# The last group without its unread state, and the two halves of the last output block in the other order

## The chip, the cores and the metric

The kernel runs on one core of a Trainium2 chip. The metric is device time in microseconds (us) of one execution: 551.74 us, the median of three runs (549.87 to 553.06). The engines are TensorE (PE: matmuls, with PEld its weight loads), VectorE (DVE), ScalarE (ACT), GpSimd (POOL) and SyncE (SP), which issues transfers. They run side by side and meet at semaphores.

## The reference

Two stages follow each other: a gated linear recurrence with complex gates, and a feed-forward layer that takes the maximum over three products. B = 4, H = 8 heads, S = 768 steps, D = 48; 3072 tokens of 384 features, 768 hidden features.

```python
mag = np.sqrt(a_re * a_re + a_im * a_im)
scale = np.minimum(mag, 0.999) / (mag + 1e-06)
a_re_n, a_im_n = (a_re * scale, a_im * scale)
for t in range(S):
    new_re = ar * S_re - ai * S_im
    new_im = ar * S_im + ai * S_re
    kv = np.einsum('bhd,bhe->bhde', k[:, :, t], v[:, :, t])
    S_re, S_im = (new_re + kv, new_im)
    y[:, :, t] = np.einsum('bhd,bhde->bhe', q[:, :, t], S_re)
x = y.transpose(0, 2, 1, 3).reshape(B * S, H * D)
h = np.maximum(np.maximum(x @ w1, x @ w2), x @ w3)
return h @ w_out
```

The state `S_re`, `S_im` is read in its own step and carried into the next; after the last step nobody reads it.

## The kernel before, in words

The 768 steps are cut into 12 groups (`NG`) of 64. A group has two units, x and y (`C` = 2), each with two of the four batch rows, 64 steps of each on one half of the 128 partitions. For a group the kernel works out the logarithms of the gates' magnitudes (`Ln`) and their angles, turns q and k by the angles, takes the products inside the group (`A`, `B`), adds what comes from the state before the group (`y` with `QG` and `gs`), and adds the group's own keys and values to the state (`dk`, `h0`, `h1`). Then comes the feed-forward layer of the group: `U01`, `U11`, `U02`, `U12` are products of 128x256 with the three weights, with the maxima `u..` behind them, and the product with `w_out` is split in Strassen's manner into seven: `S1` to `S4` are the sums before it on DVE, `P1` to `P7` the products on PE, `r1` to `r57`, `ox`, `oy`, `oz` the additions into the output tile `ot` behind it, and `Dx`, `Dy`, `Dz` the output transfers. `Px` and `Py` are the products of the one block of features that stays outside the split.

The order of everything is written out by hand in the string `SCHEDULE` (line 21): each word is a step, a colon and the group. The class `Bound` (line 189) ties every instruction of an engine to the one before it, so that each engine runs its instructions in just that order; this is also why all of them carry line 198. PSUM tiles of two banks come from `banks` (line 208), whose four slots follow the string `SLOTS` (line 116).

The steps that the change touches:

- `sums` (line 623, in `turns`): per unit, products of `Ln` with two constant matrices. `mid` gives the decay between each step and the middle of its block of eight; `rest` the decay from that middle to the end of the group. Each is four products of 64x192; all go to one PSUM tile, side by side.
- `Ek`, `Eq`, `En` (line 631): exponentials of these sums on ACT. `Ek` and `Eq` read the columns of `mid` and scale k and q (`mk`, `mq`). `En` reads the columns of `rest`.
- `kEn` (line 656): DVE multiplies the turned keys `uk` by `En`, after the transposes `tpk` have read them. The result is read by `dk` alone, the group's own share of the state. For the last group, number 11, `SCHEDULE` has no `dk`, `h0` or `h1`, but before the change it has `Eny:11`, `Enx:11`, `kEnx:11` and `kEny:11`.
- `oy` and `oz` (line 943, in `seven`): in every other group `oy` adds a PSUM bank of 384 columns into the y half's output tile. In the last group `oy` adds the lower 192 columns, into which `P4` and `Py` are summed, and `oz` the upper 192, into which only `Py` is. Both read the second bank of the tile `op7`. The upper half of `ot` is complete ahead of `oz` with `r57`, the lower half ahead of `oy` with `r7`; both of these wait for `P7`.
- `Dy` and `Dz` (`D` in `project`, line 948): the output transfers of these halves in the last group, 64 rows of 192 columns (48 KB) each on the queue of SP and on that of ACT:

```python
queue = act if ch and g == NG - 1 else sp
cols = halves if g == NG - 1 and c == 1 else slice(0, DM)
queue.dma_start(out=out[t0:t0 + L64, cols], in_=T["ot", x][ch * L64:(ch + 1) * L64, cols])
```

The end of `SCHEDULE` before the change reads:

```
u02:11 Dy:10 S3:11 P1:11 r1:11 P2:11 S1:11 S2:11 P5:11 S4:11 P6:11 kEny:11 P3:11 r6:11 r5:11 ox:11 P7:11 P4:11 r7:11
r57:11 Dx:11 oy:11 Dy:11 oz:11 Dz:11
```

The last group's `sums` stand in the middle of work on groups 8 to 10: `sumsy:11` between `dk` and `P3:8`, `sumsx:11` between `dk` and `cs:11`.

Of the kernel before, what the change touches and what calls it, by code (L numbers as in the profile page):

```python
# [97 lines left out]
g2x:9 g3x:9 S3:8 tpkx:10 u12:8 mqx:10 b1y:9 b1x:9 b0x:9 sumsy:10 F:10 Kcx:10 yx:9 S1:8 f3:10 f1:10 addw:11 Eqy:10 xx:9  # L98
h0x:9 S2:8 mqy:10 P5:8 f0:10 f2:10 QGy:9 Eky:10 uqx:10 Lvx:10 lnw:11 kEnx:9 P7:8 Lvy:10 Px:8 P2:8 P6:8 Py:8 half:11
expL:11 mulai:11 uqy:10 P4:8 r1:8 mulw:11 Eny:10 Lky:10 mky:10 r6:8 r5:8 r7:8 r57:8 Lnop:11 oy:8 yy:9 S4:8 tpqx:10  # L100
dkx:9 kEnx:10 h1x:9 xy:9 sumsy:11 stt:11 Eky:11 Cdx:10 Qcx:10 P3:8 uky:10 ox:8 atan:11 Eny:11 Lvx:11 Eqy:11 Lvy:11
U11:9 KBx:10 h0x:10 tpky:10 h0y:10 tpqy:10 Cdy:10 dkx:10 turn:11 Lqy:11 u11:9 kEny:10 Q1x:10 mqy:11 Kcy:10 dky:10
h1x:10 sumsx:11 Qcy:10 cs:11 t:11 h1y:10 nfy:11 nfx:11 F:11 f3:11 Dy:8 Q2y:10 Lqx:11 Ekx:11 U12:9 f1:11 u12:9 QGx:10
S3:9 Lkx:11 mkx:11 U01:9 Q2x:10 f2:11 Eqx:11 af:11 mqx:11 Q1y:10 u01:9 Enx:11 U02:9 QBx:10 Bx:10 Ax:10 u02:9 Ay:10
S1:9 g0x:10 f0:11 P1:9 g1x:10 sb:11 KBy:10 g2x:10 Dx:8 g3x:10 b1x:10 g0y:10 P5:9 g1y:10 Lky:11 mky:11 sa:11 P7:9
QBy:10 g2y:10 g3y:10 S2:9 Py:9 b0x:10 yx:10 xx:10 By:10 b0y:10 P6:9 QGy:10 Px:9 S4:9 P2:9 r1:9 uqy:11 r6:9 P3:9 P4:9
uqx:11 uky:11 r5:9 r7:9 b1y:10 r57:9 yy:10 ox:9 tpqy:11 oy:9 ukx:11 tpqx:11 Qcy:11 xy:10 Q2y:11 tpky:11 Qcx:11 QBx:11
tpkx:11 U01:10 Q2x:11 Q1x:11 Q1y:11 U11:10 u01:10 Kcx:11 KBx:11 Kcy:11 QGy:11 U02:10 u02:10 Bx:11 QBy:11 KBy:11 u11:10
Ax:11 Ay:11 g0y:11 By:11 Dy:9 g0x:11 U12:10 g1y:11 g2y:11 g3y:11 b0y:11 b1y:11 yy:11 S3:10 g1x:11 g2x:11 Dx:9 u12:10
g3x:11 P1:10 Py:10 QGx:11 P4:10 b1x:11 P7:10 S1:10 S2:10 b0x:11 xy:11 Py:11 P5:10 S4:10 yx:11 P6:10 xx:11 r1:10 r6:10  # L110
r5:10 kEnx:11 Px:10 Px:11 P2:10 U11:11 r7:10 r57:10 oy:10 P3:10 ox:10 U01:11 Dx:10 u11:11 U12:11 u12:11 U02:11 u01:11
u02:11 Dy:10 S3:11 P1:11 r1:11 P2:11 S1:11 S2:11 P5:11 S4:11 P6:11 kEny:11 P3:11 r6:11 r5:11 ox:11 P7:11 P4:11 r7:11
r57:11 Dx:11 oy:11 Dy:11 oz:11 Dz:11
"""

SLOTS = """
# [17 lines left out]
def kernel(  # L134
# [25 lines left out]
    NG = S // L64  # L160
# [47 lines left out]
    def banks(nm, n=None):  # L208

        ps = psum.tile([P, 2, 512], FP, tag="ps" + next(slots), name=nm)  # L210
        T["ps"] = ps
        return ps if n is None else ps.rearrange("p a n -> p (a n)")[:, 0:n]
# [4 lines left out]
    def activation(func, **kw):  # L217

        need = SETS.get(func, T.get("set"))
        if need != T.get("set"):  # L220
            act.preload_act_table_set(need)
            T["set"] = need
        act.activation(func=func, **kw)
# [5 lines left out]
    def copy(out, in_):  # L229

        if other():
            dve.tensor_copy(out=out, in_=in_)
        else:
            act.copy(out=out, in_=in_)
# [15 lines left out]
    def once(key, make):  # L250

        if key not in T:
            T[key] = make()
        return T[key]
# [12 lines left out]
    def ones(name, *shape):  # L267
        t = const.tile([P, *shape], FP, name=name)
        dve.memset(t, 1.0)
        return t  # L270
# [10 lines left out]
    mid = ones("mid", L64)  # L281

    rest = ones("rest", L64)
# [99 lines left out]
    def every(view, j):  # L383

        return view.rearrange("p (i u d) -> p i u d", u=2, d=D)[:, :, j]
# [84 lines left out]
    def two(t):  # L470
        n = t.shape[1] // D
        return t.rearrange("p (h u d) -> p h u d", u=1, d=D).to_broadcast([P, n, 2, D])

    def both(t, h):

        return t[:, h]

    def sines_of(t):

        dims = [list(d) for d in t[:, :, 0:D].ap]  # L480
        return bass.AP(t.tensor, t.offset, dims[:-1] + [[L64, 2], dims[-1]])

    def hd(t):
        return t.rearrange("p c h d -> p (c h d)")
# [135 lines left out]
    def turns(g, c, name):  # L620

        x = g * C + c
        if name == "sums":
            ps = T["sums", x] = banks("sums")
            for n, mat in enumerate((mid, rest)):
                for j in range(2):
                    for ch in range(2):
                        r = slice(ch * L64, (ch + 1) * L64)
                        mm(out=ps[j * L64:(j + 1) * L64, ch, n * HC:(n + 1) * HC], lhsT=mat[r],
                           rhs=every(T["Ln", g][r, c * DM:(c + 1) * DM], j), start=True, stop=True)  # L630
        elif name in ("En", "Ek", "Eq"):
            n, sg = {"En": (1, -1.0), "Ek": (0, 1.0), "Eq": (0, -1.0)}[name]
            E = T[name, x] = nat2.tile([P, DM], FP, tag=name[:1 + (n == 1)], name=name[:1 + (n == 1)])
            activation(out=E.rearrange("p (c n) -> p c n", c=2), in_=T["sums", x][:, :, n * HC:(n + 1) * HC],
                           func=AF.Exp, scale=sg)
        elif name in ("mk", "mq"):
            t = hd(T[name[1], x])
            dve.tensor_tensor(out=t, in0=T["E" + name[1], x], in1=t, op=OP.mult)
        elif name in ("uk", "uq"):
            u = T["U" + name[1], x] = us[name[1]][x % len(us[name[1]])]  # L640
            dve.tensor_tensor(out=sines_of(u), in0=T["CS", g][:, c], in1=two(hd(T[name[1], x])), op=OP.mult)
        elif name in ("tpk", "tpq"):
            ps = banks("tp").rearrange("p j (n t) -> p j n t", t=L64)
            T[name, x] = ps[0:DD]
            for n in range(H):
                for j in range(2):
                    r = slice(j * L64, (j + 1) * L64)
                    pe.transpose(out=ps[0:DD, j, n], in_=both(T["U" + name[2], x], n)[r], identity=ident[r, r])
        elif name == "Kc":
            T["K", x] = un2.tile([P, H, P], FP, tag="K", name="K")  # L650
            copy(out=T["K", x][0:DD].rearrange("p n (j t) -> p j n t", j=2), in_=T["tpk", x])
        elif name == "Qc":
            T["Q", x] = un2.tile([P, 4 * H, 80], FP, tag="Q", name="Q")
            copy(out=T["Q", x][0:DD, :, 0:32].rearrange("p (n j a) t -> p j n a t", n=H, j=2),
                 in_=T["tpq", x].rearrange("p j n (a t) -> p j n a t", a=2))
        elif name == "kEn":
            u = sines_of(T["Uk", x])
            dve.tensor_tensor(out=u, in0=u, in1=two(T["En", x]), op=OP.mult)
        elif name == "F":
            tile_sums(g, c)  # L660
        elif name[0] == "f" and name[1:].isdigit():
            tile_factors(g, [c], int(name[1:]))
        else:
            return False
        return True

    def tile_sums(g, c):

        ps = once(("Fp", g, c if g == 0 else "xy"), lambda: banks("F"))
        T["F", g * C + c] = fs[g % 2][:, c]  # L670
        for i in range(2):
            for j in range(2):
                for u in range(2):
                    h, o = 2 * (2 * i + u) + j, u * L64
                    for ch in range(2):
                        r = slice(ch * L64, (ch + 1) * L64)
                        at = (4 * (c if g > 0 else 0) + 2 * i + j) * NF
                        mm(out=ps[o:o + D, ch, at:at + NF],
                           lhsT=T["Ln", g][r, c * DM + h * D:c * DM + (h + 1) * D], rhs=cuts[r],
                           start=True, stop=True)  # L680

    def tile_factors(g, cs, name):

        i, u = divmod(name, 2)
        o, n = i * L64, len(cs)
        ps = T["Fp", g, cs[0] if g == 0 else "xy"][u * L64:u * L64 + D, :, 0:4 * n * NF]
        ps = ps.rearrange("p h (c i n) -> p c h i n", c=n, i=2)
        out = fs[g % 2][o:o + D, cs[0]:cs[0] + n]
        out = out.rearrange("p c (h i u) j n -> p c h i u (j n)", h=2, u=2)[:, :, :, :, u]
        if n == 1:  # L690
            out, ps = out[:, 0], ps[:, 0]
        activation(out=out, in_=ps, func=AF.Exp, scale=-1.0)
# [337 lines left out]
    for c in range(C):  # L1030
        for nm, src in (("ar", a_re), ("ai", a_im)):
            t = once((nm, 0), lambda: ld2.tile([P, C, H, D], FP, tag=nm, name=nm))
# [38 lines left out]
```

## Time and profile before

| what | value |
|---|---|
| median of 3 runs | 551.74 us |
| the runs | 551.74, 549.87, 553.06 us |
| the profiled execution | 552.02 us, its span 550.3 us |
| mean granted TensorE clock | 0.978 |
| last TensorE instruction ends | about 546.2 us in the span |
| bytes moved | 47.93 MB |

The span runs from the first to the last instruction of the profiled execution; its time holds some 1.7 us around it. In the profile's rows an operation is named by its output and inputs (`sums<-Ln,rest`), with the shape and how many of it; a product shows as two rows. The number in square brackets is the time that the engine was idle before, and what ended it; "issue" means that it waited for nothing that the profile shows. `wo` and `w` are names of the weight tiles, `strassen` the tile of the sums before the products, `xhx` the features.

### The profile page before, as it was taken

The numbers are of one execution on the slowest core, as the hardware profiler recorded it, in microseconds if no ns is written. First come the engines' busy times: TensorE is split into PE (matmuls) and PEld (weight loads), VectorE is DVE, ScalarE is ACT, GpSimd is POOL, SyncE is SP. The second block draws the span as 40 slices with busy tenths as digits, with TensorE's granted clock in tenths as the row PEclk, the third lists the DMA queues.
The fourth block names the chain that finished last, engine by engine and source line by source line (L and its number), as shares of the span: only waits on it lengthen the run. The fifth ranks groups of instructions, "written<-read, shape, count | busy, mean of one in ns | idle before, by whom it ended". The sixth has DMA issues, their size and how long they took to land.

```text
span 550.3 us, 22368 instructions
## 1 busy us (share of the span) xinstructions
PE 515.6 (94%) x9998; PEld 441.4 (80%) x9998; DVE 484.8 (88%) x735; ACT 363.8 (66%) x568; POOL 115.6 (21%) x167
## 2 busy tenths in 40 slices
PE   2478989999999999999999999999999899999996
PEld 1245578778988888988898988988988788988886
DVE  7999989999999999999999999988999687886325
ACT  6999898688989778696492638677678465221000
POOL 7524180030251222214004001303101250000000
PEclk9769899999999999999999999999999899999999
DMA  8978975553443455244516025356150350010011
GB/s 233 243 206 170 244 129 89 101 92 69 80 89 74 96 111 104 49 91 83 104 42 121 3 52 107 64 105 112 22 104 11 66 117 2 4 30 4 2 29 29
DMA packets 117023, 47.93 MB, mean 87 GB/s; under 512 B 103936, under 2 KB 109536, under 8 KB 116928
## 3 DMA queue, kind: packets, MB, share of 16 engines
q1 hardware_dynamic: 104272, 31.87, 27.4%
q0 software_dynamic: 10304, 14.05, 14.1%
q8 instruction: 78, 1.28, 0.9%
q10 hardware_dynamic: 2352, 0.59, 0.5%
q14 instruction: 17, 0.14, 0.1%
HBM read 33.03 MB, written 4.72 MB: 69 GB/s over the span
## 4 chain that ended last, share of the span: by engine, by line
PE 71%; DVE 10%; issue 2%; ACT 1%; DVEq 0%; ACTq 0%
PE up L198 28%; PE op L198 22%; PE y L198 6%; PE tp L198 4%; PE A L198 3%; PE dk L198 3%; PE sums L198 2%; DVE atm L198 1%; PE B L198 1%; DVE Q L198 1%; PE F L198 1%; DVE QG L198 1%; PE cs L198 1%; DVE uk L198 1%; DVE xhx L198 1%
## 5 line engine op out<-in xcount | busy, mean ns | idle before, releaser
L198 PE MATMUL up<-xhx,w 128*128 128x256 f32 x792 | 177.5, 382 | 0.0
L198 PEld LDWEIGHTS up<-xhx,w 128*128 128x128 f32 x792 | 148.6, 190 | 22.4 <-DVE g L198 2.2
L198 ACT ACT_TABLE_LOAD x50 | 64.2, 1283 | 4.4 <-issue 3.6
L198 POOL DMA_DIRECT2D ar<-nf x44 | 39.9, 1297 | 77.8 <-DVE ar L198 66.7
L198 ACT COPY atm<-B 32x128 f32<-32x128 f32 x96 | 24.5, 256 | 39.4 <-DVE atm L198 24.2
L198 PE MATMUL op<-wo,xhx 128*128 128x192 f32 (+1 forms) x220 | 49.2, 362 | 0.0
L198 DVE TENSOR_TENSOR Q<-Q,f 112x1024 f32<-112x1024 f32 (+1 forms) x48 | 45.3, 951 | 0.4 <-ACT Q L198 0.2
L198 PE MATMUL y<-atm,vb 128*32 128x64 f32 x1152 | 39.4, 221 | 2.9 <-issue 2.9
L198 PEld LDWEIGHTS op<-wo,xhx 128*128 128x128 f32 x220 | 36.7, 190 | 3.3 <-issue 0.6
L198 PEld LDWEIGHTS y<-atm,vb 128*32 128x32 f32 x1152 | 33.1, 110 | 7.3 <-issue 6.2
L198 PE MATMUL y<-QG,g 112*32 112x64 f32 x1408 | 37.3, 220 | 0.5 <-issue 0.5
L198 DVE TENSOR_TENSOR ot<-ot,op 128x192 f32<-128x192 f32 (+1 forms) x67 | 27.1, 413 | 11.0 <-PE op L198 6.2
L198 DVE TENSOR_TENSOR xhx<-xhx,up 128x768 f32<-128x768 f32 x22 | 20.9, 951 | 17.9 <-PE up L198 17.9
L198 PEld LDWEIGHTS y<-QG,g 112*32 112x32 f32 x1408 | 34.6, 110 | 0.7 <-issue 0.7
L198 PE MATMUL op<-wo,strassen 128*128 128x192 f32 x176 | 34.2, 339 | 0.1
L198 POOL DMA_DIRECT2D w<-L x8 | 9.0, 1124 | 117.4 <-ACT L L198 104.8
L198 PE MATMUL op<-w,strassen 128*128 128x192 f32 x176 | 32.8, 329 | 0.0
L198 DVE COPY_PREDICATED atm<-masko,A 128x256 f32<-128x256 uint8 x72 | 31.2, 435 | 1.2
L198 PEld LDWEIGHTS op<-wo,strassen 128*128 128x128 f32 x176 | 30.0, 196 | 2.3 <-issue 0.7
L198 PE MATMUL A<-Q,K 112*32 112x80 f32 x1536 | 30.6, 234 | 0.5 <-issue 0.5
L198 PEld LDWEIGHTS op<-w,strassen 128*128 128x128 f32 x176 | 28.9, 190 | 1.9 <-ACT ot L198 0.8
L198 PEld LDWEIGHTS A<-Q,K 112*32 112x32 f32 x1536 | 27.4, 110 | 3.6 <-issue 1.4
(156 smaller groups left out, 1114.5 us busy)
## 6 DMA issues: line engine op xcount, KB each, us to landing
ai<-in_a_im_dram SPq DMA_DIRECT2D x46, 96.0 KB, 3.4
ar<-in_a_re_dram SPq DMA_DIRECT2D x46, 96.0 KB, 3.3
out_dram<-ot SPq DMA_DIRECT2D x45, 96.0 KB, 3.0
Ln<-e POOLq DMA_DIRECT2D x10, 384.0 KB, 5.7
q<-in_q_dram SPq DMA_DIRECT2D x34, 96.0 KB, 3.3
k<-in_k_dram SPq DMA_DIRECT2D x32, 96.0 KB, 3.6
w<-L POOLq DMA_DIRECT2D x8, 384.0 KB, 5.0
w<-in_moe_w_dram SPq DMA_DIRECT2D x3, 768.0 KB, 7.0
```

The source lines that it names most:

```text
L198: ins = f(*a, **kw)
```

## The change

The last group's sums lose their `rest` half; its exponentials `En` and its products `kEn` are taken out of the order; and at the end `oz` and `Dz` stand ahead of `oy` and `Dy`. The lines of `SCHEDULE` are wrapped anew, without another change of order. The words taken out, with their neighbours, and the end:

```diff
-atan:11 Eny:11 Lvx:11
+atan:11 Lvx:11
...
-u01:9 Enx:11 U02:9
+u01:9 U02:9
...
-r5:10 kEnx:11 Px:10
+r5:10 Px:10
...
-P6:11 kEny:11 P3:11
+P6:11 P3:11
...
-Dx:11 oy:11 Dy:11 oz:11 Dz:11
+Dx:11 oz:11 Dz:11 oy:11 Dy:11
```

```diff
         if name == "sums":
             ps = T["sums", x] = banks("sums")
-            for n, mat in enumerate((mid, rest)):
+            for n, mat in enumerate((mid, rest) if g < NG - 1 else (mid,)):
```

On the engines that is 8 products fewer on PE, 2 exponentials fewer on ACT and 2 multiplications fewer on DVE, of 9998 rows, 568 and 735 instructions. The table loads of ACT and the orders of POOL and SP stay the same but for the two halves at the end.

More of the change, by code (lines that the diff above doesn't have):

```diff
@@ L100 @@
 expL:11 mulai:11 uqy:10 P4:8 r1:8 mulw:11 Eny:10 Lky:10 mky:10 r6:8 r5:8 r7:8 r57:8 Lnop:11 oy:8 yy:9 S4:8 tpqx:10
[L101 to L113, printed above, removed]
+dkx:9 kEnx:10 h1x:9 xy:9 sumsy:11 stt:11 Eky:11 Cdx:10 Qcx:10 P3:8 uky:10 ox:8 atan:11 Lvx:11 Eqy:11 Lvy:11 U11:9
@@ new lines @@
+KBx:10 h0x:10 tpky:10 h0y:10 tpqy:10 Cdy:10 dkx:10 turn:11 Lqy:11 u11:9 kEny:10 Q1x:10 mqy:11 Kcy:10 dky:10 h1x:10
+sumsx:11 Qcy:10 cs:11 t:11 h1y:10 nfy:11 nfx:11 F:11 f3:11 Dy:8 Q2y:10 Lqx:11 Ekx:11 U12:9 f1:11 u12:9 QGx:10 S3:9
+Lkx:11 mkx:11 U01:9 Q2x:10 f2:11 Eqx:11 af:11 mqx:11 Q1y:10 u01:9 U02:9 QBx:10 Bx:10 Ax:10 u02:9 Ay:10 S1:9 g0x:10
+f0:11 P1:9 g1x:10 sb:11 KBy:10 g2x:10 Dx:8 g3x:10 b1x:10 g0y:10 P5:9 g1y:10 Lky:11 mky:11 sa:11 P7:9 QBy:10 g2y:10
+g3y:10 S2:9 Py:9 b0x:10 yx:10 xx:10 By:10 b0y:10 P6:9 QGy:10 Px:9 S4:9 P2:9 r1:9 uqy:11 r6:9 P3:9 P4:9 uqx:11 uky:11
@@ new lines @@
+r5:9 r7:9 b1y:10 r57:9 yy:10 ox:9 tpqy:11 oy:9 ukx:11 tpqx:11 Qcy:11 xy:10 Q2y:11 tpky:11 Qcx:11 QBx:11 tpkx:11 U01:10
+Q2x:11 Q1x:11 Q1y:11 U11:10 u01:10 Kcx:11 KBx:11 Kcy:11 QGy:11 U02:10 u02:10 Bx:11 QBy:11 KBy:11 u11:10 Ax:11 Ay:11
+g0y:11 By:11 Dy:9 g0x:11 U12:10 g1y:11 g2y:11 g3y:11 b0y:11 b1y:11 yy:11 S3:10 g1x:11 g2x:11 Dx:9 u12:10 g3x:11 P1:10
+Py:10 QGx:11 P4:10 b1x:11 P7:10 S1:10 S2:10 b0x:11 xy:11 Py:11 P5:10 S4:10 yx:11 P6:10 xx:11 r1:10 r6:10 r5:10 Px:10
+Px:11 P2:10 U11:11 r7:10 r57:10 oy:10 P3:10 ox:10 U01:11 Dx:10 u11:11 U12:11 u12:11 U02:11 u01:11 u02:11 Dy:10 S3:11
@@ L114 @@
+P1:11 r1:11 P2:11 S1:11 S2:11 P5:11 S4:11 P6:11 P3:11 r6:11 r5:11 ox:11 P7:11 P4:11 r7:11 r57:11 Dx:11 oz:11 Dz:11
+oy:11 Dy:11
 """
```

## The prediction

> **What bounds the kernel now.** I read the page first, for the share of each engine, and then the busy time by stretches of the span, since the change touches only the last 105 us.
>
> ```profile
> PE 515.6 (94%) x9998; PEld 441.4 (80%) x9998; DVE 484.8 (88%) x735; ACT 363.8 (66%) x568; POOL 115.6 (21%) x167
> ```
> ```profile
> 440.00:470.00 30.00, 30.00 (x686) 26.47 (x688) 24.11 (x35) 16.23 (x23) 7.43 (x10) 1.00 0.24 55
> 470.00:500.00 30.00, 29.97 (x544) 26.86 (x537) 23.05 (x36) 7.22 (x15) 0.00 (x0) 1.00 0.07 16
> 500.00:520.00 20.00, 20.00 (x425) 17.75 (x416) 11.99 (x22) 2.85 (x10) 0.00 (x0) 1.00 0.01 2
> 537.00:547.00 10.00, 9.17 (x57) 8.82 (x55) 6.91 (x13) 0.32 (x1) 0.00 (x0) 1.00 0.07 20
> ```
>
> After the stretch and its length the columns are the busy us of PE, PEld, DVE, ACT and POOL, the granted clock, the DMA share and GB/s. Where the change acts, TensorE is busy all the time at full clock, while DVE has 20 to 40% free and ACT 46 to 86%. So an instruction taken off PE should shorten the run by its own step, and one taken off DVE or ACT should give nothing unless PE waits for it. The chain of waits says the same: from 440 us to the last product every piece but 0.05 us is PE's.
>
> ```profile
> 454.04 0.67 PE sums L198 x14
> ...
> 537.05 9.13 PE op L198 x56
> 546.18 0.02 issue
> 546.21 0.35 DVE ot L198
> 546.56 0.26 DVEq L1066
> ```
>
> Only the last two pieces belong to another engine: one addition and the hand-over to the output transfer.
>
> **Part 1a: eight `rest` products leave PE.** In the last group, each of the two `sums` runs loses its four products with `rest`; each shows as two rows. The timeline at both places:
>
> ```profile
> 444.68 0.38 PE L198 MATMUL sums<-Ln,mid 64*64 64x192 f32 x2
> 445.05 0.56 PE L198 MATMUL sums<-Ln,rest 64*64 64x192 f32 x8
> 445.54 1.27 PEld L198 LDWEIGHTS op<-wo,strassen 128*128 128x128 f32 x8 [0.28 <-issue]
> 453.77 0.38 PE L198 MATMUL sums<-Ln,mid 64*64 64x192 f32 x2
> 454.15 0.56 PE L198 MATMUL sums<-Ln,rest 64*64 64x192 f32 x8
> 454.47 0.88 PE L198 MATMUL cs<-w,upto 64*64 64x384 f32 x8
> ```
>
> The durations overlap, so the price is the distance between starts. At the second place, `rest` starts at 454.15 and what follows at 454.47: 0.32 us. The chain gives the same size: 0.67 us for 14 rows is 0.048 a row, 0.38 for eight. At the first place it is 445.54 - 445.05 = 0.49 us, but there the next work uses the whole array and its first weight load comes after a gap of 0.28, which `mid` in front of it would leave as well. There the step lies between 0.32 and 0.49. Sum: 0.64 to 0.87 us. I take 0.70, twice 0.35, since the gap should stay.
>
> **Does anything behind PE eat it?** Two places where PE is nearly met by DVE:
>
> ```profile
> 450.46 0.95 DVE L198 SCALAR_TENSOR_TENSOR w<-w,ar 128x768 f32<-128x768 f32 x1
> 451.63 0.96 DVE L198 TENSOR_TENSOR uk<-uk,En 128x768 f32<-128x768 f32 x1 [0.22 <-PE tp L198]
> 451.96 1.94 PEld L198 LDWEIGHTS dk<-vb,uk 64*64 64x64 f32 x127
> 468.01 0.95 DVE L198 TENSOR_TENSOR xhx<-xhx,up 128x768 f32<-128x768 f32 x1 [1.40 <-PE up L198]
> 474.74 0.43 DVE L198 COPY_PREDICATED atm<-masko,A 128x256 f32<-128x256 uint8 x1
> 475.29 0.19 PEld L198 LDWEIGHTS y<-atm,vb 128*32 128x32 f32 x8 [0.61 <-issue]
> 514.33 0.16 PEld L198 LDWEIGHTS y<-atm,vb 128*32 128x32 f32 x8 [0.23 <-issue]
> ```
>
> First, `kEny:10` (451.63 to 452.59) must be done before the second half of the `dk` loads, which begins at about 451.96 + 1.94/2 = 452.93. With PE 0.35 us ahead that half wants to begin at 452.58; the product can begin at 451.41, when DVE has finished the row before, and so end at 452.37. It holds, with 0.2 us to spare. Second, `y` at 475.29 follows DVE's masked copy, which ends at 475.17; here DVE is the late one, by some 0.4 us (0.61 idle against 0.23 at 514.33, where the masked copies are long done; an estimate). But DVE's row of work up to there starts with the `xhx` maximum at 468.01, which had waited 1.40 us for PE. If PE comes earlier, the whole row comes earlier. The gain passes through. Were both to fail, it would be 0, and I keep 0 as the lower end.
>
> **Part 1b: two `En` exponentials on ACT, two `kEn` products on DVE.**
>
> ```profile
> L198 ACT ACTIVATE En<-sums x24: 469/490/502, 25.1 to 464.8; 128x384 f32<-128x384 f32 x24
> ```
> ```profile
> 518.67 0.95 DVE L198 TENSOR_TENSOR uk<-uk,En 128x768 f32<-128x768 f32 x1
> 540.64 1.33 PEld L198 LDWEIGHTS op<-w,strassen 128*128 128x128 f32 x8
> 541.61 0.95 DVE L198 TENSOR_TENSOR uk<-uk,En 128x768 f32<-128x768 f32 x1
> 541.94 1.33 PEld L198 LDWEIGHTS op<-wo,strassen 128*128 128x128 f32 x8
> 542.48 0.74 DVE L198 TENSOR_TENSOR ot<-ot,op 128x192 f32<-128x192 f32 x2
> 543.27 1.30 PEld L198 LDWEIGHTS op<-w,strassen 128*128 128x128 f32 x8
> ```
>
> (First row: shortest, median and longest duration in ns, first and last start.) ACT sheds 2 x 0.49 = 0.98 us and DVE 1.90. The table loads beside the exponentials stay, since other exponentials of the same set stand there. All of it is covered: the `En` by the `up` products that keep PE busy in the stretch 440 to 470, the `kEn` at 518.67 by PE's steady products up to 537. The one at 541.61 is the closest call: it makes `r6` and `r5` end at 543.22, and P7, whose weights load at 543.27, waits for `r5` by the built instruction list. P3's loads, at 541.94, start 1.33 us before P7's; P6's, at 540.64, start 1.30 before P3's. So at most 0.03 us of that wait is on the path: upper end 0.03, taken as nothing. If that cover were gone, each `kEn` would be worth its full 0.95.
>
> **Part 2: `oz` and `Dz` ahead of `oy` and `Dy`.** The rows of the tail:
>
> ```profile
> 544.70 1.46 PE L198 MATMUL op<-w,xhx 128*128 128x192 f32 x8
> 544.90 0.74 DVE L198 TENSOR_TENSOR ot<-ot,op 128x192 f32<-128x192 f32 x2 [0.74 <-PE op L198]
> 546.21 0.62 DVE L198 TENSOR_TENSOR ot<-ot,op 128x192 f32<-128x192 f32 x2 [0.56 <-PE op L198]
> 546.59 1.10 SPq L198 DMA_DIRECT2D out_dram<-ot  x2
> 546.59 1.38 ACTq L198 DMA_DIRECT2D out_dram<-ot  x2
> ```
>
> P4 runs from 544.70 to 546.16, `r7` and `r57` from 544.90 to 545.64, then `oy` and `oz` back to back in 0.62 us, then on each of two queues the 48 KB of `Dy` and of `Dz`. By its data, `oz` needs only `Py` and `r57` and could run at 545.64, beside P4. But the built instruction list of the changed kernel has, as DVE's last additions (`oz`, then `oy`):
>
> ```
> TensorTensor ot_7806<-ot_7806,op_7644 128x192 [waits DVE_49,PE_49]
> TensorTensor ot_7806<-ot_7806,op_7644 128x192
> ```
>
> `oz` waits for TensorE's count 5384, which P4's last product sets; `oy` behind it has no wait left. The wait goes by the PSUM tile into which P4 writes and from which `oz` reads, not by the columns. So the two additions change places, both still after P4; both transfers are 48 KB on the same queues in the same order of places. `Dz` starts where `Dy` did and the other way round. Part 2 is worth 0.
>
> The Trainium skill speaks against getting more here: PSUM — Partial Sum Buffer, section "PSUM bank collisions raise a hardware error", has semaphores guard by bank and quadrant, since two engines in one collide even at other columns. `oz` reads the upper columns of the bank into which P4 writes, so by that rule the wait cannot be dropped; no run here shows a collision. By a view of the data alone the tail would be 0.5 us shorter (rival A).
>
> **The sum.** -0.70 (PE) + 0 (ACT, DVE) + 0 (tail) = -0.70 us against the profiled execution's own 552.02 us (span 550.3): 551.3. That execution lies 0.28 above the median of the runs, 551.74, so for a median I forecast 551.0 us, 0.13% faster. Over 0.5%, 2.76 us, is about what a measurement of this kernel can tell from no change, so this counts as within.
>
> **The rivals.**
>
> A. *`oz` slips ahead of P4 after all.* `Dz` is issued from about 546.0 under P4, and `Dy` at 546.59 is the last, where before the second transfer was issued at 546.59 + 1.10/2 = 547.14. That is 0.55 more: 551.0 - 0.55 = 550.5. For it speaks the data, against it the wait in the list. Chance 0.05.
>
> B. *The gain is absorbed at 452.6 or 475.3* because DVE does not come earlier. Then nothing is left: 551.7. Against it speaks the 1.40 us that DVE waited for PE at 468.01. Chance 0.10.
>
> C and D rest on a stall that the trace has just ahead of the change:
>
> ```profile
> 430.41 0.11 PEld L198 LDWEIGHTS y<-atm,vb 128*32 128x32 f32 x2 [2.76 <-issue]
> ```
> ```profile
> 428.00:430.00 2.00, 0.00 (x0) 0.00 (x0) 0.96 (x2) 1.03 (x2) 0.00 (x0) 1.00 0.96 163
> 431.00:435.00 4.00, 4.00 (x76) 3.83 (x66) 2.60 (x3) 2.56 (x5) 0.00 (x0) 0.57 0.11 21
> ```
>
> In the middle of a row of `y` products PE has nothing to issue for 2.76 us while the DMA engines are 96% busy, and the clock granted in the 4 us afterwards is 0.57, which loses 4 x 0.43 = 1.7 us of full-speed time. Together 4.5 us. No data are waited for, so I read it as instructions that arrive late behind the transfers. (The Trainium skill, Runtime: NRT & Kernel Launch, section "Instruction fetch mechanics", has each engine's stream come in blocks by DMA, which fits the row.)
>
> C. *Slower:* PE's stream is shorter from 444.9 on, so every later block falls at another point of the work. If one falls under a burst of transfers as at 428, the price is 4.5: 551.0 + 4.5 = 555.5. It decides only where the DMA share stays near 0.96 for some 3 us; after 440 the stretches show 0.24, 0.07 and 0.01. Chance 0.06.
>
> D. *Faster:* the stall at 428 itself is missing or shorter. The stream ahead of it is the same, so nothing in the change does this, but its length can differ from run to run, and the runs lie 3.2 us apart. 551.0 - 4.5 = 546.5. Chance 0.09.
>
> **How the numbers follow.** Range: the lowest run before, 549.87, less 0.9 (the upper end of the sum), 549.0; the highest, 553.06, less 0.6 (the lower price of the rows), 552.5. It holds the forecast, A at 550.5 and B at 551.7, and leaves out C and D, 0.15. The forecast itself has 0.70. Faster by over 0.5% is D, 0.09; slower by over 0.5% is C, 0.06; the rest, 0.85, is within.
>
> **What would show it.** In the changed profile: no `rest` row after 440 us, `op` starting 0.3 to 0.4 us after the last `mid` row of the first place and `cs` likewise at the second; from there every PE piece 0.7 us earlier, measured from the same piece ahead of 444 us (for instance the `up` row after the stall). `oz` starting before P4's end would prove A. `y` near 475 still at 475.29 would prove B. A PE gap of over 1 us after 445, or none at 428, would be C or D, and would make the forecast wrong although its steps held.

## The result, and the profile after

| | before | after |
|---|---|---|
| median (17 runs each) | 550.90 us | 552.95 us |
| lowest and highest run | 548.69, 553.06 | 550.92, 556.94 |
| ratio after to before, 95% interval | | 1.0040 [1.0023, 1.0057] |
| the profiled execution, its span | 552.02, 550.3 us | 553.76, 552.0 us |

The change costs 1.3 to 3.1 us (the interval, times 551), where the forecast was a gain of 0.7. The instructions taken out are gone. From the page of after, the busy time of the engines and the row of the instruction queue (the transfers that bring the engines' own instructions):

```profile
PE 512.5 (93%) x9982; PEld 439.2 (80%) x9982; DVE 483.8 (88%) x733; ACT 363.2 (66%) x566; POOL 114.4 (21%) x167
...
q8 instruction: 78, 1.28, 1.0%
```

PE has 16 rows of products and 16 of weight loads fewer (9998 each before), DVE and ACT two instructions each. PE is busy 3.1 us less, and yet the run is longer: it must be idle for longer. Where, the chain of waits says. From after, each piece with start, length and what it is:

```profile
441.80 1.72 PE y L198 x112
...
445.19 0.34 PE sums L198 x6
...
451.95 1.88 PE dk L198 x106
453.83 0.77 issue
454.60 0.37 PE dk L198 x8
...
455.03 0.34 PE sums L198 x6
...
500.05 2.12 PE A L198 x120
502.17 0.83 issue
503.00 0.35 PE A L198 x8
503.35 0.29 PE B L198 x30
...
547.91 0.02 issue
```

The same chain of before, at the same places:

```profile
441.57 1.72 PE y L198 x112
...
444.95 0.67 PE sums L198 x14
...
452.04 1.95 PE dk L198 x119
...
499.39 2.22 PE A L198 x126
501.61 0.30 PE B L198 x27
```

Two new gaps stand in the chain of after, in the middle of the row of `dk` and of the row of `A`, both put down to "issue": no data are waited for. As a ruler for all runs I take the *last part*, from the `y` piece of 112 rows near 441 us to the 0.02 us of issue behind the last product. Before it lasts 546.18 - 441.57 = 104.61 us, after 547.91 - 441.80 = 106.11. The difference of 1.50 us is made up of:

- first `sums` run: 0.34 instead of 0.67, so -0.33;
- second `sums` run: 0.34 instead of 0.67, so -0.33;
- `dk`: from its start to the second `sums` run 455.03 - 451.95 = 3.08 instead of 454.04 - 452.04 = 2.00, so +1.08;
- `A`: from its start to `B` 503.35 - 500.05 = 3.30 instead of 501.61 - 499.39 = 2.22, so +1.08.

Sum -0.66 + 2.16 = +1.50. The remaining 0.23 us of the two profiled executions (441.80 against 441.57) arose ahead of the change. It is the net of two larger differences: PE comes to the old stall in the row of `y` 1.85 us later (its loads go on at 432.26 instead of 430.41, behind the same 2.76 us of idle time), and from there to 441 us it needs 1.62 us less. The change touches neither stretch, and executions differ by more than that.

**What the gaps have in common.** The instruction queue moved 1.28 MB in 78 packets, so 16.4 KB each. PE's instructions are 2 x 9982 = 19,964 rows, and 19,964 / 78 = 256: the packets are PE's instructions in blocks of 256. This is an inference from the count, and the distances below bear it out. (The Trainium skill, Runtime: NRT & Kernel Launch, section "Instruction fetch mechanics", gives the same block of 16 KiB and 256 instructions.) The old stall in the row of `y` is there in after too. From its timeline, weight loads of PE, with start, length, shapes, count, and the idle time in front:

```profile
432.26 0.11 PEld L198 LDWEIGHTS y<-atm,vb 128*32 128x32 f32 x2 [2.76 <-issue]
```

If blocks are the cause, this stall and the two new gaps lie a whole number of blocks apart. The busy time by stretches of after, cut at the three gaps:

```profile
430.00:453.85 23.85, 21.56 (x509) 19.34 (x510) 19.32 (x29) 13.54 (x20) 9.18 (x12) 1.00 0.43 93
454.55:502.20 47.65, 47.55 (x893) 42.33 (x892) 35.75 (x52) 14.04 (x25) 0.00 (x0) 1.00 0.05 11
```

Products and weight loads together are 509 + 510 = 1019 and 893 + 892 = 1785 rows. PE's stream also holds semaphore instructions, which these columns leave out: the trace of after lists 5 between the first two gaps and 7 between the next. With them the counts are 1024 and 1792, exactly four and seven blocks. So all three gaps lie at the same place of their block. Counted in this way from the start of the trace, the rows behind the three gaps have 16,321, 17,345 and 19,137 rows ahead of them, each 193 more than a multiple of 256. The same holds in all fourteen traces: from 100 us to the last product, every gap of over 0.2 us between PE's products and loads stands at a count that is 193 more than a multiple of 256.

In before, `dk` and `A` also cross a block boundary, with no gap. What differs is when the block arrives. From the DMA view of before, in the stretch 495.75 to 496.50, the instruction queue with its packets:

```profile
q8 instruction: 1, 0.02, 7.7%
```

From the DMA view of after, in the stretch 500.25 to 501.00, all packets and those of the instruction queue:

```profile
DMA packets 1, 0.02 MB, mean 22 GB/s; under 512 B 0, under 2 KB 0, under 8 KB 0
...
q8 instruction: 1, 0.02, 8.9%
```

In before the packet for `A` runs during the large `up` products ahead of it, some 3 us before `A` starts (499.39). In after there is none between 495.75 and 496.50; it runs only once `A` itself does (from 500.05), 2.0 to 2.75 us before PE goes on at 503.00, on DMA engines with nothing else to do. For `dk` likewise: one packet between 449.50 and 450.25 in before, in after none there and one between 451.75 and 452.00, 2.6 to 2.85 us ahead of 454.60. A packet thus needs some 2.0 to 2.85 us until its instructions run; the small products of `dk` and `A` use up 256 instructions in about that time (1.95 us for 119 product rows and as many loads, `dk` before). A packet that starts during the slow `up` is in time; one that starts during the small products is late. The other block boundaries say the same. From 100 us on the fourteen traces have 972 of them. At none does the first instruction run less than 2.17 us after the start of its packet; the median is 5.4. At 66 PE has a gap of over 0.15 us, and at 64 of these the time from packet to instruction is 2.17 to 2.80 us (the other two are 3.04, in e8, and 3.55, the stall in `y` of e9).

### The profile page after: what moved, and what is told of

Its sections match the earlier page's. It is cut to its first block, busy times and chain, and to the rows that moved or that the text cites. A ratio compares the mean times of both kernels' runs of the same rounds, so it can differ in the third digit from the quotient of the medians.

```text
span 552.0 us, 22332 instructions
## 1 busy us (share of the span) xinstructions
PE 512.5 (93%) x9982; PEld 439.2 (80%) x9982; DVE 483.8 (88%) x733; ACT 363.2 (66%) x566; POOL 114.4 (21%) x167
## 3 DMA queue, kind: packets, MB, share of 16 engines
q8 instruction: 78, 1.28, 1.0%
## 4 chain that ended last, share of the span: by engine, by line
PE 71%; DVE 10%; issue 2%; ACT 1%; DVEq 0%; ACTq 0%
PE up L198 28%; PE op L198 22%; PE y L198 6%; PE tp L198 3%; PE A L198 3%; PE dk L198 3%; PE sums L198 2%; DVE atm L198 1%; PE B L198 1%; DVE Q L198 1%; PE F L198 1%; DVE QG L198 1%; PE cs L198 1%; DVE uk L198 1%; DVE xhx L198 1%
## 5 line engine op out<-in xcount | busy, mean ns | idle before, releaser
L198 PE MATMUL op<-wo,strassen 128*128 128x192 f32 x176 | 33.0, 331 | 0.1
```

The lines of the kernel that those rows point to most:

```text
L198: ins = f(*a, **kw)
```

## The experiments

The theories, as they stood:

- **T**: the phase of the blocks. Taking out 32 instructions moves every later block boundary in the work, and where one falls in rows of small products, PE waits about 1 us for its block.
- **R1**: the edits on ACT and DVE or the new order of the tail cost the time.
- **R2**: the gaps come by chance with any new build.
- **R3** (added after e5 to e9, on record from e10 on): any shift of PE's stream costs, so that T explains nothing in particular about these two places.

None of the kernels changes an output. All ratios are against the kernel before, run beside each on the same chip, with 95% intervals.

| run | PE instructions against before | ratio | gap in `dk`, `A` | last part, us |
|---|---|---|---|---|
| after | -16, then -32 | 1.0040 [1.0023, 1.0057] | 0.77, 0.83 | 106.11 |
| e1_keep_rest | 0 | 0.9995 [0.9978, 1.0013] | none | 104.61 |
| e2_pad_late | 0 | 0.9988 [0.9965, 1.0010] | none | 104.14 |
| e3_rest_only | -16, then -32 | 1.0046 [1.0024, 1.0068] | 1.12, 1.05 | 106.68 |
| e4_tail_only | 0 | 0.9987 [0.9971, 1.0004] | none | 104.61 |
| e5_before_start8 | +32 from the start | 1.0174 [1.0143, 1.0206] | none (1.26 in `op`) | 106.18 |
| e6_before_start56 | +224 from the start | 1.0269 [1.0242, 1.0295] | 1.16, 0.81 | 107.10 |
| e7_after_start8 | +32, then +16 and 0 | 1.0116 [1.0093, 1.0140] | none | 103.96 |
| e8_after_start24 | +96, then +80 and +64 | 1.0376 [1.0345, 1.0407] | none (1.83 in `B`, 0.62 in `F`) | 107.50 |
| e9_pad_mid | +32 from 408 us, then +16 and 0 | 1.0041 [1.0014, 1.0067] | none | 103.96 |
| e10_first_only | -16, then -16 | 1.0024 [1.0000, 1.0048] | 0.76, none | 105.34 |
| e11_second_only | 0, then -16 | 0.9999 [0.9980, 1.0019] | none | 104.29 |
| e12_pad_first | 0, then -16 | 0.9988 [0.9963, 1.0013] | none | 104.18 |

"Then" gives the shift behind the first and the second place of the missing `rest` products. At the boundary in `dk` only the first place lies behind, at that in `A` both.

### One part at a time: e1, e3, e4

e1 is the changed kernel with the `rest` products back (nobody reads them; the other edits stay):

```diff
-            for n, mat in enumerate((mid, rest) if g < NG - 1 else (mid,)):
+            for n, mat in enumerate((mid, rest)):
```

> The changed kernel with the eight rest products of the last group kept; the exponentials, the DVE products and the order at the end stay as changed. Theory T (PE's instruction stream is 32 instructions shorter, so the points at which the next block of instructions is asked for fall 32 instructions later in the work, and two of them land in dense small products at 453.8 and 502.2 us, 1.08 us each): no stall at either place, ratio to the kernel before 1.000 +- 0.001. Rival R1 (the lighter ACT and DVE work or the new order at the end costs the time): both stalls stay and the ratio is 1.003 to 1.004. Rival R2 (the slower time is a spread between builds, not tied to any place): no reason for the stalls at just these places to go; the ratio may be anything within 0.995 to 1.005.

Its chain of waits at the two places:

```profile
452.43 1.95 PE dk L198 x119
...
499.78 2.23 PE A L198 x127
```

Both rows in one piece, and a last part of 104.61, that of before. So everything but the missing products leaves the last part as it was; by time it is worth nothing that the interval shows, 0.9978 to 1.0013.

e3 is the other half: the kernel before without the `rest` products alone. `En` reads the columns of `mid` in the last group, and `kEn` and the tail stay as they were; this only alters the unread state.

```diff
-            for n, mat in enumerate((mid, rest)):
+            for n, mat in enumerate((mid, rest) if g < NG - 1 else (mid,)):
...
+            n = n if g < NG - 1 else 0
```

> The kernel before with only the eight rest products of the last group taken out; the two exponentials stay and read the columns of mid, the DVE products and the order at the end stay as before (the product of the last group's keys with the exponential is still read by nobody). Theory T: both stalls as in the changed kernel, 0.77 to 0.9 us each in the timeline, ratio 1.003 +- 0.0015. R1: no stalls, and the forecast gain, ratio 0.9987.

The chain of e3:

```profile
453.93 1.87 PE dk L198 x108
455.80 1.12 issue
456.92 0.37 PE dk L198 x8
...
502.38 2.12 PE A L198 x120
504.50 1.05 issue
505.55 0.35 PE A L198 x8
```

Both gaps are back, at the same rows (8 `dk` and 8 `A` rows behind them, as in after), and so is the time: 1.0046. They are longer than the 0.77 to 0.9 us that were expected. e1 and e3 together put all of the loss on the missing products, which R1 cannot explain.

e4 is the kernel before with the order `oz Dz oy Dy` alone:

```diff
-r57:11 Dx:11 oy:11 Dy:11 oz:11 Dz:11
+r57:11 Dx:11 oz:11 Dz:11 oy:11 Dy:11
```

> The kernel before with only the order at the end changed (oz, Dz ahead of oy, Dy). The prediction: oz still waits for P4, the two additions change places, ratio 1.000 +- 0.001, oz not before the end of P4. Rival A of the prediction: oz ahead of P4's end and 0.55 us less, ratio 0.999.

The timeline of its tail:

```profile
543.04 1.46 PE L198 MATMUL op<-w,xhx 128*128 128x192 f32 x8
...
544.55 0.62 DVE L198 TENSOR_TENSOR ot<-ot,op 128x192 f32<-128x192 f32 x2 [0.56 <-PE op L198]
```

`P4` ends at 543.04 + 1.46 = 544.50, and both additions still come behind it, at 544.55. The last part ends with the last product and can't show the order behind it; from there to the end of the span e4 takes 548.7 - 544.52 = 4.2 us and before 550.3 - 546.18 = 4.1. The new order brings nothing there, where rival A promised 0.55.

### The work taken out, the phase kept: e2

e2 is the changed kernel with eight `rest` products again, but of 4 columns instead of 192, into columns that nobody reads. PE's stream has before's length, the work almost that of after.

```diff
+                        m = 1 if n and g == NG - 1 else D
...
-                        mm(out=ps[j * L64:(j + 1) * L64, ch, n * HC:(n + 1) * HC], lhsT=mat[r],
-                           rhs=every(T["Ln", g][r, c * DM:(c + 1) * DM], j), start=True, stop=True)
+                        mm(out=ps[j * L64:(j + 1) * L64, ch, n * HC:n * HC + 4 * m], lhsT=mat[r],
+                           rhs=every(T["Ln", g][r, c * DM:(c + 1) * DM], j)[:, :, 0:m], start=True, stop=True)
```

> The changed kernel, with eight rest products of 4 columns in place of 192 at the same two places, written to PSUM and read by nobody: PE's stream has the length of before, with next to none of the work. Theory T: no stall at 453.8 and 502.2, and the saving forecast for the products comes out: 0.4 to 0.7 us less than before, ratio 0.9987 to 0.9993. R1: both stalls stay, ratio 1.003. R2: anything.

The chain of e2 at the two places:

```profile
450.25 1.95 PE dk L198 x115
...
497.39 2.23 PE A L198 x127
```

No gap, and a last part of 104.14 (from 440.04 to 544.18), 0.47 below before. With the count of instructions restored, the saving that the change was to bring appears, by two thirds. The interval of the ratio lies below that of after and holds 1: this is better than the changed kernel, and not told from before by time.

### The phase shifted, the last group untouched: e6, with e5, e7, e8

These put one-column products into a free column of the PSUM tile of `F`, ahead of the first group's first product; nobody reads them. Each is 4 instructions. e5 and e6 are the kernel before with 8 and 56 of them, e7 and e8 the changed kernel with 8 and 24:

```diff
+        for _ in range(8 if g == 0 and c == 0 else 0):
+            mm(out=ps[0:L64, 0, 511:512], lhsT=mid[0:L64], rhs=mid[0:L64, 0:1], start=True, stop=True)
```

> The kernel before with 56 products of one column (224 PE instructions) ahead of its first product: modulo 256 instructions this is the changed kernel's phase in the last part (32 fewer), with the last group's work untouched. Theory T: gaps of 0.8 to 1.2 us in the dk products near 453 and the A products near 502, though no step of the change is made; the last 105 us from the second y product of group 10 take 106.5 to 106.9 us in place of 104.61. Rival R2: no gap there, 104.6.

+224 is -32 within a block of 256. So e6 has before's work, at `A` after's phase, and at `dk` a phase 16 instructions beyond it (after has -16 there). Its chain:

```profile
463.39 1.99 PE dk L198 x111
465.38 1.16 issue
466.54 0.25 PE dk L198 x2
...
512.20 2.10 PE A L198 x119
514.30 0.81 issue
515.11 0.36 PE A L198 x9
```

Its busy time by stretches, cut at its gap in `y` (439.02 to 442.00), in `dk` and in `A`:

```profile
439.10:465.40 26.30, 23.38 (x510) 21.07 (x509) 19.64 (x29) 13.85 (x21) 9.19 (x12) 0.94 0.39 85
466.50:514.30 47.80, 47.73 (x892) 42.54 (x893) 35.74 (x52) 14.44 (x26) 0.00 (x0) 1.00 0.05 11
```

Not one step of the last groups differs from before, and the gaps are there, with the same 1019 and 1785 rows between them as in after, and 5 and 7 semaphore instructions again. This is the run that tells T from R1 and, with e3, from R2. The last part, 107.10, is a little over what was expected. The ratio of 1.0269 is not all phase: the 56 products take 12.0 us, and `pw`, which follows the first group's `F`, starts at 15.34 instead of 11.56, so that up to 3.8 of the 14.8 us lost are the padding's own time. The 8 and the 24 products of the other runs end by 7.9 us, before `F` starts.

> The kernel before with 8 products of one column (32 PE instructions) ahead of its first product, while PE waits 10.8 us for POOL's constants; their output is read by nobody. Everything later on PE stands 32 instructions later in the stream. Theory T: the block that was late for the y products at 427.6 us is now asked for before the products ahead of it, some 7 us earlier, so the 2.5 to 2.8 us stall there and the 0.57 clock of the 4 us behind it go: 4 to 4.5 us less, ratio 0.992 +- 0.002, unless the new phase hits another place, which then shows as a gap inside a row of small products. Rival R2 (stalls belong to the work at that place, or to the transfers alone): the stall at 428 stays, ratio 1.000.

Missed. The stall in `y` near 428 goes, but the whole run loses 1.7%, and gaps open elsewhere. From the timeline of e5, weight loads:

```profile
103.22 4.36 PEld L198 LDWEIGHTS up<-xT,w 128*128 128x128 f32 x24 [2.07 <-issue]
...
431.40 3.75 PEld L198 LDWEIGHTS up<-xhx,w 128*128 128x128 f32 x18 [1.17 <-issue]
```

I had counted only the stall that I knew; a shift at the start moves all boundaries, 78 or 79 of them. This gave rise to R3.

> The changed kernel with the same 8 one-column products at the start: its last part is back in the phase of before, the rest is shifted by 32. Theory T: no gaps at 453 and 502, the last part 0.65 us shorter than before (103.9 to 104.0 in place of 104.61), the stall at 428 gone as in the kernel before with the same 8; ratio to the kernel before 0.991 +- 0.002. Rival R2: stalls as in the changed kernel, ratio 1.003.

The chain of e7 at the two places:

```profile
458.18 1.95 PE dk L198 x119
...
505.21 2.23 PE A L198 x127
```

e7 brings `A` back to before's phase and `dk` to 16 instructions beyond it, and both gaps go: last part 103.96, 0.65 below before, which is the price of the `rest` products. R3, though put down later, falls here, for the last part: this shift costs nothing there. The expected ratio was missed by the same cause as in e5, gaps ahead of the last part.

> The changed kernel with 24 one-column products (96 instructions) at the start: another phase, to see whether the first was a lucky one. Theory T: the stall at 428 gone (its block is asked for long before), the last part between 103.9 and 105.0; gaps elsewhere only inside rows of small products; ratio 0.988 to 0.999. Rival R2: ratio 1.003, gaps at 428, 453 and 502.

Missed as well, and it shows the size of the stake. The stall in `y`, which was to go, is there with 2.88 us (79 product rows further on than in after: at +96, the next boundary falls some 160 instructions later). The last part is 107.50 where at most 105.0 was expected. The chain of e8, the stall and a gap in the row of `B`:

```profile
444.60 2.88 issue
...
494.00 1.83 issue
```

The ratio is 1.0376 where after's is 1.0040: 0.0336 x 551 = 18.5 us for 96 instructions that delay no step at the start (`F` starts at 10.53, in after at 10.95). Added up from 100 us on, the gaps of over 0.15 us at block boundaries are 16.0 us in the profiled execution of e8 and 4.9 in that of after; that is 11 of the 18.5, and the rest isn't traced. Of the phases tried from the start, before's is the best.

### Shifted only from 408 us on: e9

The changed kernel with eight one-column products behind the `sums` of unit x in group 10; they are not read.

```diff
+            for n in range(8 if x == 2 * (NG - 2) else 0):
+                j, ch = n // 2 % 2, n % 2
+                r = slice(ch * L64, (ch + 1) * L64)
+                mm(out=ps[j * L64:(j + 1) * L64, ch, 511:512], lhsT=mid[r], rhs=mid[r, 0:1], start=True, stop=True)
```

> The changed kernel with 8 one-column products (32 PE instructions, output read by nobody) right behind the sums of unit x of group 10, some 18 us ahead of the stall at 428. So PE's stream is 32 instructions later only between about 408 us and the last group's sums, where the rest products left out take the 32 back; before and behind it the phase is that of before. Theory T: the gap of 2.5 to 2.8 us in y with the 0.57 clock behind it (4.2 us together) is replaced by one of about 1 us ahead of the up products, as with the 8 at the start; none at 453 and 502; the last part 103.9 to 104.1. Sum: -0.65 - 4.2 + 1.0 + 0.2 = -3.6 us, ratio 0.993 +- 0.002. Rival R2 (the phase counts only by chance, or the long gap belongs to the transfers): the gap in y stays, ratio 0.999.

The chain of e9 around the old stall:

```profile
420.48 1.06 issue
421.55 4.15 PE up L198 x18
...
429.10 0.24 PE y L198 x4
429.34 4.14 issue
```

Behind it the row without gaps of e7 appears, last part 103.96. Ahead of it a gap opens in front of `up`, as expected; the stall in `y` does not go but moves by 16 product rows (4 ahead of it, 20 in after), which is 32 instructions, and grows to 4.14 us. That it sits on the boundary is shown once more; the saving upstream was a miss. It also shows that the phase alone does not decide: e5 and e7 have the same phase at this boundary and no gap there.

### One place at a time: e10, e11, e12

The changed kernel with `rest` taken out at one place only: e10 at the first (unit y), e11 at the second (unit x). e12 is e11 with the products of 4 columns, as in e2, at the first place.

```diff
-            for n, mat in enumerate((mid, rest) if g < NG - 1 else (mid,)):
+            for n, mat in enumerate((mid, rest) if g < NG - 1 or c == 0 else (mid,)):
```

(e10; e11 and e12 have `c == 1`, and e12 the lines of e2.)

> The changed kernel with the rest products left out at the first place (unit y) alone, so 16 PE instructions fewer from there on in place of 32. Theory T with lead: PE's sequencer runs some way ahead of the array, and ahead of slow up products this lead is worth 0.11 us an instruction. In the kernel before, the block that dk needs was asked for at 449.75 and in the changed one at 451.75, both 2.85 us ahead of its use at the earliest; PE gets there near 453.7. With half the shift it is asked for near 450.75, and ready near 453.6: no gap in dk, or one under 0.3; none in A. The last part 104.2 to 104.6 (before 104.61, changed 106.11). Rival R3 (any shift of the phase costs about 1 us a place, no lead in it): gaps of 0.7 to 1.1 at dk and A, last part 106 and more.

The chain of e10:

```profile
453.34 0.76 issue
...
499.87 2.23 PE A L198 x126
```

The gap in `dk` stays, against what I expected. The mistake was mine: only the first place lies ahead of `dk`, so e10 shifts that boundary just as far as after does. The last part, 105.34, is over the 104.2 to 104.6 expected by that gap. At `A` it shifts by 16 instead of 32, and there the gap is gone. So 16 are enough for a gap at `dk` and too few for one at `A`.

> The changed kernel with the rest products left out at the second place (unit x) alone: 16 PE instructions fewer from 454 on. Theory T with lead: dk stands as before (no gap); the block for A, asked for at 496.0 before and at 500.5 in the changed kernel, is asked for near 498.2 and is ready before A's end near 501: no gap; the last part 104.2 to 104.4. Rival R3: a gap of 0.8 to 1.0 in A, last part 105.2 to 105.4.

> The changed kernel with four rest products of 4 columns (read by nobody) in place of 192 at the first place alone, none at the second: the phase is that of before up to 454 us and 16 instructions off from there, where neither the half change nor the kernel before showed a gap. Theory T: no gap in dk or A, the last part 103.9 to 104.1 in place of 104.61, ratio 0.9985 to 0.9992; the best of both kernels, though its 0.6 us may not stand clear of the spread of the runs. Rival R2: gaps at 453 or 502 again, last part over 105.

The chain of e11 at the second place (`dk` is in one piece too, of 1.95 us):

```profile
498.93 2.23 PE A L198 x127
```

No gap in either run; last part 104.29 (104.61 - 0.32, one place's worth) and, for e12, 104.18, a little over the 104.1 expected. In e12 the block in `dk` comes just in time: 2.24 us from the packet to its first instruction. By ratio e2 and e12 are at 0.9988, with 1 inside the interval, level with e4 (0.9987), which saves nothing in the last part. Each beats the changed kernel, whose interval begins at 1.0023; that e2 and e12 beat before is seen in the last part (by 0.47 and 0.43 us) and not resolved by time. e7 and e9 show the full 0.65 us in the last part, and lose it upstream.

## Why the prediction was wrong, point by point

- **Part 1a, -0.70 (0.64 to 0.87).** Right. Measured -0.33 and -0.33 in the chain, -0.32 in e11, -0.65 in e7. The gap ahead of `op` stayed, as assumed.
- **"Does anything behind PE eat it?"** At the two places named, nothing did; the pass of `dk` and `y` by DVE held (e7, e9). But the question was asked only of other engines. What ate the gain sits on PE itself: how its own instructions arrive.
- **Part 1b, 0, and Part 2, 0.** Right: e1 has the last part of before, 104.61, and in e4 `oz` still stood behind `P4`, with the same time behind the last product (4.2 us against 4.1). Rival A falls with e4, B with e7. D did not come: the stall of 2.76 us is there in after.
- **The step that failed is rival C's.** Its mechanism is the one that happened: a shorter stream, blocks at other points. But the prediction let it decide "only where the DMA share stays near 0.96 for some 3 us", priced it at 4.5 us and gave it 0.06. The condition was read off one stall that happened to lie under a burst, and the runs show that it is not needed: the gap in `A` opened at a DMA share of 0.02 (500.05 to 503.00), with no packet under way but that of the block itself. (At `dk` transfers were under way, a share of 0.48 from 451.95 to 454.60, so `A` is the clear case.) What decides in the runs is whether the packet of the block starts during slow products or during small ones, which use up a block about as fast as the next comes. So there were more places for a gap than the prediction counted, each cheaper: 1.08 us rather than 4.5, and two of them, 2.16, against a gain of 0.66. The range, which left C out, did not hold the result. Neither gap reaches the 1 us by which the prediction would have known C (0.77 and 0.83 in the chain). That the time still lies within 0.5% of before, to which it gave 0.85, is luck as far as the mechanism goes: other shifts of PE's stream moved the time by 1.2 to 3.8% (e5 to e8).
- **Could it be had from the trace of before?** The place could: 1024 and 1792 instructions behind the stall at 428 us lie in `dk` and in `A`, rows of small products (61 and 57 product rows per microsecond, where `up` has 4.6), so those two boundaries deserved a look. Whether 32 instructions were enough to make them late could not; e10 and e11 show that it hangs on 16.
- **Open:** what exactly triggers the request for a block. In before the packet for the `y` stall goes out after 427.75, only 2.66 us or less ahead of the resumption at 430.41, and no run tells why so late. In e9 the packet for this boundary starts 8.4 us after PE went on behind the boundary before it, in e7, with the same phase, 4.6 us; in the 4 us ahead of it the DMA share is 0.83 in e9 and 0.02 in e7. That the transfers hold up the request there is possible and not shown. What the traces do show is that from 100 us on no packet starts with more than 298 rows of PE's stream still ahead of its first instruction, so at the start of a packet PE never has much more than one block left to run. The whole difference by time, 1.3 to 3.1 us, holds the 1.50 of the last part; whether anything upstream adds to it isn't known. The two profiled executions show little there: ahead of the last part, from 100 us on, the gaps of over 0.15 us at block boundaries add up to 3.1 us in before and 3.4 in after.

## What to carry to other kernels

Where one engine is busy all the time with thousands of small instructions, count its instructions in blocks of 256 from a known stall, and look at every boundary that lies in a row of small ones: a gap marked "issue" there is likely a block that came late, not a wait for data; a packet of the instruction queue some 2 to 3 us ahead of its end says so. Semaphore instructions count too. The gap can also stand at the first rows of large products straight behind small ones, as in `up` of e9 and `op` of e5. Taking work out of such an engine shifts all later boundaries; make the cut without changing the count (small products in place of large ones), or find out on the chip what the new phase costs. In this kernel, a time that moved by less than about 2 us after an edit to PE's stream says little about the edit until the gaps are read.

## What the runs showed of the hardware that was not expected

- **The phase of the blocks is worth 11 us and more in 550.** The Trainium skill, Runtime: NRT & Kernel Launch, section "Instruction fetch mechanics", calls the crossing of a block mostly hidden. Of 78 blocks most are, but the gaps at single ones in the chains above are 0.62 to 4.14 us long, and kernels with 32 to 224 instructions more at the start lie 1.2 to 3.8% above before (e7, e5, e6, e8; in e6 up to 3.8 us of it is the padding's own time).
- **The same stall, another clock.** The stall in `y` is 2.76 us on the weight loads in both profiled executions. Busy time by stretches, the 4 us behind it, of before:

```profile
430.45:434.45 4.00, 4.00 (x99) 3.83 (x100) 2.04 (x3) 2.01 (x5) 0.00 (x0) 0.62 0.25 48
```

and of after:

```profile
432.30:436.30 4.00, 4.00 (x108) 3.91 (x109) 2.44 (x3) 2.40 (x5) 0.00 (x0) 1.00 0.24 47
```

The granted clock (the third value from the end) is 0.62 in the one and 1.00 in the other, which fits the 1.62 us that after gains between the stall and 441 us. The 1.7 us that the prediction added for the clock is no fixed part of such a gap, and behind the gaps in `dk` and `A` it was not paid at all (1.00 in the stretch from 454.55 and from 503.00 to 507.00).
